# Thresholds of the first 28 steps on VectorE, and tails and second-batch units turned at other steps

## The chip, the cores and the metric

The kernel runs on one core of a Trainium2 chip. The metric is the device time of one execution in microseconds. The numbers here are the median of three runs, and one further execution that the hardware profiler recorded.

## The reference

An attention with a threshold feeds a two-layer perceptron. There are 8 batches of 8 heads, 576 positions and head size 64; q, k and v are float32.

```python
scores = scale * np.matmul(q, k.transpose(0, 1, 3, 2))
thresh = np.max(scores, axis=-1, keepdims=True) - tau
scores = np.where(scores >= thresh, scores, -1000000000.0)
scores = scores - np.max(scores, axis=-1, keepdims=True)
attn = np.exp(scores)
attn = attn / (np.sum(attn, axis=-1, keepdims=True) + 1e-09)
attn_out = np.matmul(attn, v)
# heads side by side: x is 4608 tokens by 512
h = x @ w_in            # 512 by 2048
out = np.maximum(0.01 * h, h) @ w_out   # 2048 by 512
```

So every row of scores needs its maximum, then the comparison with maximum minus tau, the exponential and the row's sum.

## The kernel before, in words

**Steps.** The attention is cut into 144 steps, 18 for each batch. A step handles one pair of heads and 128 queries against all 576 keys. Sixteen of the 18 are main steps: two blocks of 256 queries, four pairs of heads, two halves of the block. The last two take the 64 tail queries (positions 512 to 575) of two pairs each. Everything is issued by one loop over the step number n (lines 544 to 609); each engine has its own queue and runs what the loop gives it in that order. There is no other planner: where something is to happen at a given step, a table keyed by n holds it (`loads_at`, `pool_at`, `turns_at`, `rows_at`).

**One step on the engines.** PE multiplies the scores (line 252) into two PSUM tiles, one a head. VectorE (DVE) copies them to SBUF with the sign turned and keeps each row's least value, which is minus the maximum (line 260, tile `s`, `mn`). The threshold, `mn` plus tau, is a tiny instruction on 128x2 elements (`threshold`, lines 264 to 273): on VectorE it is line 269, and on GpSimd (POOL) line 272. One round of the loop later, ScalarE (ACT) computes, for head 0, an exponential (line 295), and for head 1 a Prelu with the threshold as bias and then an exponential (lines 291 and 292). VectorE multiplies head 0's exponential with the comparison against the threshold (`weights`, line 304). So line 291 and line 304 wait for the threshold. In round n VectorE's queue holds the copies of step n, then the threshold of step n where it is VectorE's, then the weights of step n-1.

**From weights to output.** For each two steps, VectorE takes the reciprocal of the sums (line 310), POOL spreads it over 128 columns (`widen`, line 313), and SyncE (SP) issues one transposing DMA for weights and reciprocals together (line 321). In the first eight steps PE transposes instead. Three to five steps later PE multiplies with v (`pv`, line 348), and VectorE scales the result (line 370, 360 in tail steps). After four pairs the 256 tokens go through the first layer (line 391, PSUM tile `hp`, emptied by ACT in line 393) one eighth a round, and then the second (line 407, two pieces a round at most).

**Splitting and turning q and k.** For precision, q and k are scaled by 64 and split into a high and a low float16 half, and both halves are transposed. A main unit is one pair's 512 positions of q or k; a tails unit is the 64 last positions of all pairs. For most units, POOL scales (line 137), casts (line 143) and subtracts (line 151); `turn` (line 171) lets PE transpose both halves into PSUM (line 186), and VectorE or ACT copies the result to SBUF (line 195 for main units, 189 for tails). For k tails of the second batch POOL makes one more copy (line 191). In the first two batches these run as whole units at steps that the code names; from the third batch on, another form (`turn_rows`) is used.

**PSUM banks that bind.** The tag `h` has two buffers, and `hp`, the transposes of `turn` and a part of the early transposes take them in turn. A new user waits until the one before the last has been emptied.

**What sets the order around the change.** The steps of the second batch's ten units stand in a list in line 450; the split is issued by POOL three and two rounds ahead (lines 452 to 454) and the turn at the round itself (line 456). Units come in the order k and q of pair 0, k tails, k and q of pairs 1, 2 and 3, q tails. The first batch's last units stand in lines 531 to 537: its q tails are split at round 11 and turned at round 13, and first read at step 16. In a round the first entry of `pool_at` is issued ahead of the threshold and the widen, the others behind (lines 566 to 577). The loads of w_in and w_out are in the same table (line 534).

Of the kernel before, what the change touches and what calls it, by code (L numbers as in the profile page):

```python
# [37 lines left out]
def kernel(  # L38
# [35 lines left out]
    def load_main(b, s, which, eng=None, parts=1):  # L74
        t = sb.tile([128, 4, 256], FP32, tag="raw", bufs=4, name="raw")
        n = 4 // parts
        for i in range(parts):
            (eng or nc.sync).dma_start(
                out=t[:, ds(n * i, n), :],
                in_=SRC[which][b, ds(4 * s + n * i, n), 0:MAIN, :].rearrange("h (p t) d -> p h (t d)", t=4))  # L80
        raws[b, s, which] = t

    def load_tails(b, which, engs=(nc.sync, nc.sync)):
        t = sb.tile([128, 2, 2, 64], FP32, tag="rawt", bufs=2, name="rawt")
        src = SRC[which][b, :, MAIN:S, :].rearrange("(u sh) p d -> u p sh d", u=2)
        for u in range(2):
            engs[u].dma_start(out=t[ds(64 * u, 64), :, :, :].rearrange("p s h d -> p (s h) d"), in_=src[u])
        tails[b, which] = t
# [40 lines left out]
    def split_scale(key):  # L129
        t = sb.tile([128, 4, 2, 64], FP32, tag="scaled", bufs=2, name="scaled")  # L130
        if key[1] == "t":
            src = tails[key[0], key[2]][:, :, :, :]
            dst = t[:, 0:2, :, :]
        else:
            src = pair_of(*key)
            dst = t[:, :, :, :].rearrange("p t h d -> p h t d")
        nc.gpsimd.tensor_scalar(out=dst, in0=src, scalar1=64.0, scalar2=1.0, op0=AX.mult, op1=AX.mult)  # L137
        scaled[key] = t

    def split_high(key):  # L140
        n = 2 if key[1] == "t" else 4
        halves[key] = new_half()
        nc.gpsimd.tensor_copy(out=halves[key][:, 0, 0:n, :, :], in_=scaled[key][:, 0:n, :, :])  # L143

    def split_low(key):

        n = 2 if key[1] == "t" else 4
        m = 2 if key[0] < 2 else n
        src = scaled.pop(key)
        for i in range(0, n, m):  # L150
            nc.gpsimd.tensor_tensor(out=halves[key][:, 1, i : i + m, :, :], in0=src[:, i : i + m, :, :],  # L151
                                    in1=halves[key][:, 0, i : i + m, :, :], op=AX.subtract)
# [18 lines left out]
    def turn(key, copy=None, bank="h"):  # L171
        copy = copy or nc.scalar.copy
        b, p, which = key
        dst, half = turned_of(b, which), halves.pop(key)
        n = 2 if p == "t" else 4
        c0 = 0 if which == "q" else 64
        if p == "t":
            c0 = MAIN if which == "q" else 0
            tp = ps.tile([128, 2, 2, 2, 64], FP16, tag=bank, bufs=2 if bank == "h" else 1, name="tp")
        else:  # L180
            tp = ps.tile([128, 2, 4, 128], FP16, tag="h", bufs=2, name="tp")
        for x in range(2):
            for t in range(n):
                for h in range(2):
                    o = tp[ds(64 * h, 64), x, :, t, :] if p == "t" else tp[ds(64 * h, 64), x, t, :]
                    nc.tensor.transpose(o, half[:, x, t, h, :], ident[:, :])  # L186
        if p == "t":
            src = tp[:, :, :, :, :].rearrange("d x u s p -> d x (u s) p")
            copy(out=dst[:, :, :, ds(c0, 64)], in_=src)
            if which == "k" and b:  # L190
                nc.gpsimd.tensor_copy(out=dst[:, :, :, 576:640], in_=dst[:, :, :, 0:64])
            elif which == "k":
                nc.vector.tensor_copy(out=dst[:, :, :, 576:640], in_=src)
        else:
            copy(out=dst[:, :, p, ds(c0, 512)], in_=tp[:, :, :, :].rearrange("d x t p -> d x (t p)"))
# [67 lines left out]

    def threshold(st):
        st.th = sb.tile([128, 2, 2], FP32, tag="th", bufs=3, name="th")
        if st.n < 9 or 15 <= st.n < 23:

            least = sb.tile([128, 1], FP32, tag="least", bufs=2, name="least")
            nc.vector.tensor_scalar(out=st.th[:, :, 0], in0=st.mn[:, :, 0], scalar1=tau_f, scalar2=None, op0=AX.add,
                                    op1=AX.min, accum_out=least[:, :])  # L270
        else:
            nc.gpsimd.tensor_scalar(out=st.th[:, :, 0], in0=st.mn[:, :, 0], scalar1=1.0, scalar2=tau_f, op0=AX.mult,  # L272
                                    op1=AX.add)
# [157 lines left out]
    def at(d, n, f):  # L431
        d.setdefault(n, []).append(f)

    def units(b):
        u = [(b, p, w_) for p in range(NP) for w_ in "kq"]
        return u[:2] + [(b, "t", "k")] + u[2:] + [(b, "t", "q")]
# [3 lines left out]
    for b in range(1, B):  # L440
        base = PERB * (b - 1)
        for i, (s, w_) in enumerate(((0, "k"), (0, "q"), (1, "k"), (1, "q"))):
            at(loads_at, base + ((-2, 0, 5, 7)[i] if b > 1 else (3, 4, 8, 9)[i]),
               lambda b=b, s=s, w_=w_: load_main(b, s, w_))
        for i, w_ in enumerate("kq"):
            at(loads_at, base + (1, 3)[i] if b > 1 else (6, 16)[i], lambda b=b, w_=w_: load_tails(b, w_))
        for i, key in enumerate(units(b) if b == 1 else ROWS):
            n_ = base + (5, 7, 9, 9, 11, 13, 15, 17, 19, 21)[i]
            if b == 1:
                n_ = (11, 12, 13, 14, 16, 17, 19, 20, 21, 22)[i]  # L450
            key = (b,) + key[-2:]
            at(pool_at, n_ - 3, lambda key=key: split_scale(key))
            at(pool_at, n_ - 3, lambda key=key: split_high(key))
            at(pool_at, n_ - 2, lambda key=key: split_low(key))
            if b == 1:
                at(turns_at, n_, lambda key=key, i=i: turn(key, nc.vector.tensor_copy if i < 7 else None))
            else:
                at(rows_at, n_, key)
# [47 lines left out]
    def split_pool(key):  # L506
        split_scale(key)
        split_high(key)
        split_low(key)
# [8 lines left out]
    first = units(0)  # L518
# [8 lines left out]
    for key in first[4:6]:  # L527
        split_high_act(key)
        split_scale(key)
        split_low(key)  # L530
    for n_, key in zip((1, 2, 11), first[7:]):
        at(pool_at, n_, lambda key=key: split_pool(key))
    for i in range(8):
        at(pool_at, i if i < 2 else 1 + i // 2 if i < 6 else i, lambda i=i: load_w(i))
    at(turns_at, 0, lambda: turn(first[3], nc.vector.tensor_copy))
    for n_, key in zip((1, 2, 3, 13), first[5:8] + first[9:]):
        at(turns_at, n_, lambda key=key: turn(key, nc.vector.tensor_copy if key[2] == "q" else None))

    N = len(steps)
# [4 lines left out]
    while n < N + 7 or l1q or l2q or stores:  # L544
# [12 lines left out]
        if n == 0:  # L557
            threshold(steps[0])
# [10 lines left out]
        if 0 < n < N:  # L569
            threshold(steps[n])  # L570
# [72 lines left out]
```

## Time and profile before

| what | value |
|---|---|
| median of 3 runs | 496.63 us (495.94 to 497.31) |
| profiled execution | 495.9 us |
| span of its instructions | 494.1 us |
| PE busy | 476.1 us, 96% of the span |
| VectorE (DVE) busy | 406.9 us, 82% |
| ScalarE (ACT) busy | 433.0 us, 88% |
| GpSimd (POOL) busy | 317.5 us, 64% |
| thresholds on POOL (line 272) | 127 rows, 445 ns each in the mean |
| thresholds on VectorE (line 269) | 17 rows of 0.14 to 0.16 us |
| weights (line 304) | 144 rows, 840 ns each in the mean |

Busy time is the time in which an engine executes instructions; the idle time in front of a row is put down to what released it. The share of a whole span hides that the first 100 us have other limits than the rest, so these are read in windows. The profiled execution's 495.9 us hold 1.8 us outside the span, and lie 0.73 us under the median.

### The profile page before, as it was taken

The numbers are of one execution on the slowest core, as the hardware profiler recorded it, in microseconds if no ns is written. First come the engines' busy times: TensorE is split into PE (matmuls) and PEld (weight loads), VectorE is DVE, ScalarE is ACT, GpSimd is POOL, SyncE is SP. The second block draws the span as 40 slices with busy tenths as digits, with TensorE's granted clock in tenths as the row PEclk, the third lists the DMA queues.
The fourth block names the chain that finished last, engine by engine and source line by source line (L and its number), as shares of the span: only waits on it lengthen the run. The fifth ranks groups of instructions, "written<-read, shape, count | busy, mean of one in ns | idle before, by whom it ended". The sixth has DMA issues, their size and how long they took to land.

```text
span 494.1 us, 19699 instructions
## 1 busy us (share of the span) xinstructions
PE 476.1 (96%) x8039; PEld 344.5 (70%) x8039; DVE 406.9 (82%) x1195; ACT 433.0 (88%) x784; POOL 317.5 (64%) x545
## 2 busy tenths in 40 slices
PE   8888699999999999999999999999999999999996
PEld 7666467667677777777777777777777777667884
DVE  5999698998989898999989898988989898788100
ACT  6999699999999999999999999999999999999431
POOL 5968789877866786667766677677767683222000
PEclk9999899999999999999999999999999999999999
DMA  8998798999999999989997998979988988768512
GB/s 255 262 209 148 144 165 168 207 190 171 238 176 161 224 217 182 184 183 228 156 212 162 220 195 191 211 146 217 180 203 162 200 147 161 124 123 166 106 45 66
DMA packets 220444, 87.79 MB, mean 178 GB/s; under 512 B 190656, under 2 KB 217280, under 8 KB 220352
## 3 DMA queue, kind: packets, MB, share of 16 engines
q1 hardware_dynamic: 217120, 82.00, 81.2%
q0 software_dynamic: 2688, 4.19, 4.9%
q8 instruction: 63, 1.03, 0.8%
q10 hardware_dynamic: 544, 0.33, 0.2%
q14 instruction: 29, 0.24, 0.1%
HBM read 36.70 MB, written 9.44 MB: 93 GB/s over the span
## 4 chain that ended last, share of the span: by engine, by line
PE 81%; DVE 8%; ACT 6%; POOL 2%; issue 1%; DMA 1%; DVEq 0%; POOLq 0%
PE hp L391 26%; PE sc L252 20%; PE o L407 20%; PE pv L348 7%; DVE s L260 4%; PE osc L407 3%; PE tpr L207 3%; DVE w L304 2%; ACT w L292 2%; DMA wT<-w 1%; ACT s L291 1%; ACT e L295 1%; POOL half L151 1%; PE tp L186 1%; PE idle L515 1%
## 5 line engine op out<-in xcount | busy, mean ns | idle before, releaser
L260 DVE TENSOR_SCALAR_CACHE_REDUCE s<-sc 128x576 f32<-128x576 f32 x288 | 206.4, 754 | 35.1 <-PE sc L252 32.7
L391 PE MATMUL hp<-x,win 128*64 128x256 f16 x2048 | 137.6, 277 | 1.1 <-ACT g L393 0.8
L252 PE MATMUL sc<-kT,qT 64*128 64x288 f16 (+1 forms) x1920 | 135.2, 286 | 3.1 <-DVE s L260 1.8
L391 PEld LDWEIGHTS <-win 128*64 128x64 f16 x2560 | 119.2, 110 | 24.5 <-issue 18.5
L407 PE MATMUL o<-wout,g 128*64 128x512 f16 x992 | 127.8, 379 | 0.0
L272 POOL TENSOR_SCALAR th<-mn 128x2 f32<-128x2 f32 x127 | 56.5, 445 | 108.0 <-DVE s L260 80.2
L304 DVE SCALAR_TENSOR_TENSOR w<-s,th,e 128x576 f16<-128x576 f32 x144 | 120.9, 840 | 1.5 <-POOL th L272 1.0
L252 PEld LDWEIGHTS <-qT 64*128 64x128 f16 (+1 forms) x1920 | 76.7, 97 | 57.0 <-issue 41.3
L292 ACT ACTIVATE w<-s,minus_tau 128x576 f16<-128x576 f32 x144 | 111.6, 775 | 4.9
L291 ACT ACTIVATE s<-s,th 128x576 f32<-128x576 f32 x144 | 110.3, 766 | 4.3 <-POOL th L272 3.9
L295 ACT ACTIVATE e<-s,mn 128x576 f16<-128x576 f32 x144 | 110.2, 765 | 1.1 <-DVE s L260 1.1
L393 ACT ACTIVATE g<-hp 128x512 f16<-128x512 f32 x144 | 83.9, 583 | 28.2 <-PE hp L391 27.7
L151 POOL TENSOR_TENSOR half<-scaled,half 128x512 f16<-128x512 f32 (+1 forms) x91 | 88.9, 984 | 2.2
L407 PEld LDWEIGHTS <-g 128*64 128x64 f16 x1152 | 65.3, 110 | 29.8 <-issue 0.2
L348 PE MATMUL pv<-wT,v 128*64 128x256 f16 (+1 forms) x960 | 52.1, 247 | 0.6 <-DMA wT<-w 0.5
L348 PEld LDWEIGHTS <-v 128*64 128x64 f16 x960 | 41.3, 111 | 14.5 <-DVE s L260 1.0
L137 POOL TENSOR_SCALAR scaled<-raw 128x512 f32<-128x512 f32 x62 | 45.1, 728 | 5.3 <-DMA raw<-in_k_dram 4.0
L143 POOL CAST half<-scaled 128x512 f16<-128x512 f32 (+1 forms) x74 | 42.7, 577 | 4.5
L313 POOL CAST w<-rec 128x256 f16<-128x256 f32 (+1 forms) x70 | 31.4, 449 | 12.5 <-DVE rec L310 11.7
L106 POOL CAST v<-vraw 128x256 f16<-128x256 f32 x64 | 31.7, 524 | 1.3
L370 DVE TENSOR_TENSOR x<-pv,wT 128x256 f16<-128x256 f32 x64 | 27.0, 422 | 4.6 <-PE pv L348 3.9
L292 ACT ACTIVATION_READ_ACCUMULATOR w<-s,minus_tau 128x1 f32 x144 | 26.9, 187 | 0.0
(55 smaller groups left out, 320.9 us busy)
## 6 DMA issues: line engine op xcount, KB each, us to landing
vraw<-in_v_dram SPq DMA_DIRECT2D x16, 512.0 KB, 5.1
out_dram<-osb SPq DMA_DIRECT2D x16, 512.0 KB, 3.3
raw<-in_k_dram SPq DMA_DIRECT2D x14, 512.0 KB, 4.6
raw<-in_q_dram SPq DMA_DIRECT2D x14, 512.0 KB, 4.9
win<-in_moe_w_in_dram POOLq DMA_DIRECT2D x4, 512.0 KB, 7.3
wout<-in_moe_w_out_dram POOLq DMA_DIRECT2D x4, 512.0 KB, 13.8
wT<-w SPq DMA_TRANSPOSE x68, 6.0
raw<-in_k_dram SPq DMA_DIRECT2D x4, 256.0 KB, 4.6
```

The source lines that it names most:

```text
L151: nc.gpsimd.tensor_tensor(out=halves[key][:, 1, i : i + m, :, :], in0=src[:, i : i + m, :, :], in1=halves[key][:, 0, i : i + m, :, :], op= ...
L252: nc.tensor.matmul(out=o, lhsT=lhs, rhs=turned[st.b, "k"][rows, kx, pair, ds(key0, 288)], start=(i == 0), stop=(i == 2), skip_group_check= ...
L260: nc.vector.tensor_scalar(out=st.s[:, h, :].rearrange("p (a b) -> p a b", a=2), in0=st.sc[h][:, :, 0:288], scalar1=-1.0 / UNIT, scalar2=No ...
L272: nc.gpsimd.tensor_scalar(out=st.th[:, :, 0], in0=st.mn[:, :, 0], scalar1=1.0, scalar2=tau_f, op0=AX.mult, op1=AX.add)
L291: nc.scalar.activation(out=z, in_=z, func=AF.Prelu, bias=st.th[:, h, 0:1], scale=-1.0, alpha=1e20)
L292: nc.scalar.activation(out=st.w[h], in_=z, func=AF.Exp, bias=minus_tau[:, :], scale=1.0, accum_out=st.sum[h])
L295: nc.scalar.activation(out=st.e[:, :], in_=st.s[:, h, :], func=AF.Exp, bias=st.mn[:, h, 0:1], scale=-1.0)
L304: nc.vector.scalar_tensor_tensor(out=st.w[0], in0=st.s[:, 0, :], scalar=st.th[:, 0, 0:1], in1=st.e[:, :], op0=AX.is_le, op1=AX.mult, accum ...
L348: nc.tensor.matmul(out=o, lhsT=v16[st.b % 2][:, 2 * c + u if st.tail else st.p, blk, :], rhs=rhs, start=(i == 0), stop=(i == 4), skip_grou ...
L391: nc.tensor.matmul(out=hp[ds(64 * u2, 64), jj, :], lhsT=w_in16[:, i, ds(128 * j + 64 * u2, 64)], rhs=g.x[:, i, :], start=(i == 0), stop=(i ...
L393: nc.scalar.activation(out=g.g[:, ds(nj * u, nj), :], in_=hp[:, :, :], func=AF.Prelu, bias=0.0, scale=1.0, alpha=0.01)
L407: nc.tensor.matmul(out=g.o[ds(64 * u2, 64), :], lhsT=g.g[:, j, ds(128 * m + 64 * u2, 64)], rhs=w_out16[:, j, :], start=(j == 0), stop=(j = ...
```

## The change

Three things are changed, and only in numbers of steps. The thresholds of steps 9 to 14 and 23 to 27 go from POOL to VectorE, so that VectorE has all of the first 28. The first batch's q tails are split at round 7 instead of 11 and turned at round 10 instead of 13. Of the second batch's units, k tails turn at round 14 instead of 13, k of pair 1 at 15 instead of 14, q of pair 1 at 17 instead of 16 and k of pair 2 at 18 instead of 17; their splits on POOL move with them, by one round each.

```diff
     def threshold(st):
         st.th = sb.tile([128, 2, 2], FP32, tag="th", bufs=3, name="th")
-        if st.n < 9 or 15 <= st.n < 23:
+        if st.n < 28:
...
             if b == 1:
-                n_ = (11, 12, 13, 14, 16, 17, 19, 20, 21, 22)[i]
+                n_ = (11, 12, 14, 15, 17, 18, 19, 20, 21, 22)[i]
...
-    for n_, key in zip((1, 2, 11), first[7:]):
+    for n_, key in zip((1, 2, 7), first[7:]):
         at(pool_at, n_, lambda key=key: split_pool(key))
...
-    for n_, key in zip((1, 2, 3, 13), first[5:8] + first[9:]):
+    for n_, key in zip((1, 2, 3, 10), first[5:8] + first[9:]):
         at(turns_at, n_, lambda key=key: turn(key, nc.vector.tensor_copy if key[2] == "q" else None))
```

The number of instructions is the same but for the thresholds: a threshold on VectorE also has a read of its accumulator. The order on ACT and on SP does not change. On POOL, eleven thresholds go, the first batch's q tails stand ahead of the last load of w_out, and the four moved units stand one round later.

## The prediction

> **What bounds the kernel now.** I read the page first, then the chain that ended last, then the busy time of each engine in windows, and then the timeline of each engine around the one window that differs.
>
> ```profile
> span 494.1 us, 19699 instructions
> PE 476.1 (96%) x8039; PEld 344.5 (70%) x8039; DVE 406.9 (82%) x1195; ACT 433.0 (88%) x784; POOL 317.5 (64%) x545
> ...
> PE 81%; DVE 8%; ACT 6%; POOL 2%; issue 1%; DMA 1%; DVEq 0%; POOLq 0%
> ```
>
> PE carries the kernel. In the chain in order of time, though, VectorE and ScalarE hold most of the first 73 us; from "73.47 PE sc L252" on it is nearly all PE, and the windows from 108 to 456 us show PE full. So work that gets PE to that point earlier shortens the whole, and the first 73 us are where this change acts. Windows there (columns: length; busy time of PE, PEld, DVE, ACT, POOL; granted clock; DMA share; GB/s):
>
> ```profile
> 40.00:50.00 10.00, 9.05 (x147) 6.95 (x145) 9.78 (x25) 8.93 (x16) 9.10 (x16) 1.00 0.78 134
> 50.00:60.00 10.00, 6.18 (x90) 4.35 (x86) 6.26 (x18) 6.24 (x11) 7.73 (x15) 0.83 0.83 141
> 60.00:72.00 12.00, 11.12 (x213) 8.58 (x210) 11.78 (x39) 11.56 (x21) 9.47 (x13) 1.00 0.80 153
> ```
>
> Around it DVE is 98% busy and sets the pace. In 50 to 60 us every engine loses a third. The timelines of POOL, ACT, PE and DVE (start, length, engine, line, what, idle before):
>
> ```profile
> 48.30 0.91 POOL L137 TENSOR_SCALAR scaled<-rawt 128x256 f32<-128x256 f32 x1
> 49.27 0.40 POOL L143 CAST half<-scaled 128x256 f16<-128x256 f32 x1
> 49.76 1.92 POOL L151 TENSOR_TENSOR half<-scaled,half 128x256 f16<-128x256 f32 x3
> 51.76 0.19 POOL L272 TENSOR_SCALAR th<-mn 128x2 f32<-128x2 f32 x1
> ```
> ```profile
> 51.99 0.78 ACT L291 ACTIVATE s<-s,th 128x576 f32<-128x576 f32 x1 [2.28 <-POOL th L272]
> ```
> ```profile
> 49.96 0.42 PE L186 MATMUL tp<-ident,half 128*64 128x128 f16 x8
> 54.20 0.41 PE L186 MATMUL tp<-ident,half 128*64 128x128 f16 x8 [3.81 <-ACT g L393]
> 54.54 1.62 PE L252 MATMUL sc<-kT,qT 64*128 64x288 f16 x12
> 56.09 1.92 PE L391 MATMUL hp<-x,win 128*64 128x256 f16 x16
> ```
> ```profile
> 51.99 1.27 DVE L304 SCALAR_TENSOR_TENSOR w<-s,th,e 128x576 f16<-128x576 f32 x1 [0.99 <-POOL th L272]
> 54.65 0.42 DVE L189 COPY qT<-tp 128x512 f16<-128x512 f16 x1 [1.05 <-PE tp L186]
> 56.27 0.76 DVE L260 TENSOR_SCALAR_CACHE_REDUCE s<-sc 128x576 f32<-128x576 f32 x1 [1.20 <-PE sc L252]
> ```
>
> Read as one chain: at step 12 POOL stands behind the q tails' split (L137, L143, one L151), so the threshold comes at 51.76, though its minimum was there by 48; ACT's Prelu and DVE's weights wait for it; ACT's g, behind the Prelu, empties an h bank 2.3 us late; the second tail transpose of step 13 needs that bank, so PE stands 3.81 us. Then its rows are slow: 12 score matmuls take 1.62 us (0.91 elsewhere) and 16 hp matmuls 1.92 (1.06), at a mean granted clock of 0.83.
>
> The Trainium skill (TensorE: Matmul & The Clock Gate, Part 1) says that an idle window of about 3.4 us halves PE's clock until a busy one has passed. The 3.81 us and the slow rows agree.
>
> **The change part by part.** I price on DVE, which sets the pace up to step 20, from the start of one step's first L260 copy to the next: step 9 at 38.38, 10 at 40.77, 43.60, 46.35, 49.48, 14 at 56.27, 59.98, 62.74, 65.97, 69.10, 71.99, and 20 at 74.88. That is 36.50 us for eleven steps. Costs by start-to-start times: the two copies 1.35 (38.38 to 39.73); reciprocal 0.09; weights L304 0.74 to 1.2; a main unit's copy L195 0.60 (45.75 to 46.35); 128x512 L189 or L370 0.34.
>
> *Thresholds 9 to 14 to DVE.* Alone, one delays L304 by 0.20 (36.25 to 36.45 at step 8, nothing at step 9); behind a reciprocal 0.10 (67.33 to 67.52 against 44.95 to 45.04). Even steps 0.20, odd 0.10, but step 10's copies waited 0.22 for PE, which covers step 9's. POOL loses six rows (0.19 to 0.62) and the waits for DVE before them; ACT's 0.67 and 2.28 and DVE's 0.99 waits on them go.
>
> *First batch's q tails, 11 to 7 (split) and 13 to 10 (turn).* POOL's scale 0.40, cast 0.40 and subtract about 0.7 enter the 3.86 us that it stands before its row at 35.12; the raw tails were issued by 10.2 us and landed within 9.4. The last w_out load, on POOL's queue behind them, starts 1.6 us later, at about 32; its first reader is the o row at 69.18. The eight transposes (0.3) go to PE in step 10, where PE waits for DVE at the next scores anyway; the copy adds 0.34 to DVE there. SP's order is as before.
>
> *Second batch's units.* k tails go from 13 to 14, k pair 1 to 15, q pair 1 to 17, k pair 2 to 18, each with scale, cast, subtracts and transposes, the tails with their POOL copy L191 too. Earliest reader: step 18 for the tails, 20 for pair 1, 22 for pair 2. On POOL the k tails' cast now stands behind step 11's widen, which waits for a reciprocal near 45.6; POOL can afford that wait there. No step then has two turns, so the bank conflict is gone. DVE's copies move with them.
>
> Steps 9 to 19 afterwards: 2.39; 2.83+0.20+0.34 = 3.37; 2.75+0.10 = 2.85; 3.13+0.20 = 3.33; step 13 without turns would be 1.35+0.19+0.74..1.19, but ACT needs about 2.75 a step (its e, s, w and g rows 0.68+0.80+0.78+0.48; its e rows at 46.23 and 48.94 lie 2.71 apart), so 2.75; step 14: 1.35+0.20+0.74+0.34+0.34 = 2.97; step 15: 1.35+0.19+0.98+0.60 = 3.12; step 16 on ACT again 2.75; 3.13; 2.89+0.60 = 3.49; 2.89. Sum 33.04 against 36.50: **3.46 us gained at step 20**. PE has room: its fullest step, 18, holds 0.84 scores, 0.99 hp, 0.47 tp, 0.86 o and 0.65 pv = 3.81, and step 19, without hp and pv, gives that back.
>
> *What is late next.* POOL, no longer held up, is full from about 56 us: its copy L191 waits for DVE's k tails copy of step 14 (53.1+1.35+0.20+0.82+0.34, near 55.9), and all of k pair 2 now lies behind that. From there L191 0.6, q pair 1's subtracts 1.3, a widen 0.4, k pair 2 1.1+0.7+1.5 and q pair 2 0.7+0.7+1.6 bring it to 64.5, so step 17's widen (L313) starts 1.1 us behind its reciprocal (before: at once) and ends near 64.9. The transpose issued there took 7.56 us to land, against 7.64 to its pv at 75.63: no slack. The pv of step 20 then falls at about 72.2 and the data at 72.5: 0.25 lost, between 0 and 1.5 (L151's spread 1.3 to 1.9 over three units).
>
> *Thresholds 23 to 27 to DVE.* DVE is full only in 25 to 27 (90.60 to 99.16). There 0.1+0.2+0.1 delays the pv evacuation that PE waits 0.42 for at 96.34, about 0.3. But POOL's widen of step 27 stood behind a threshold (97.99, then 98.24), the transpose behind it landed 0.52 late for PE at 105.83, and without that threshold it starts about 0.25 earlier. I take 0; ends -0.5 (the whole wait goes) and +1.0 (five at 0.20, all on the path).
>
> *Unseen: meetings of L304 with POOL.* L304 takes 0.81 clear of POOL's L137 and L143 and 1.02 to 1.27 over them. In the eleven steps it sums to 10.9 us; all clear it would be 8.9, all at 1.27 14.0: ends -2.0 and +3.1. By my row-by-row placing step 9 meets more and 10, 12 and 13 less; I take 0.
>
> Sum: 3.46 - 0.25 = **3.2 us**. The profiled execution took 495.9 us (span 494.1 and 1.8 around it), so 492.7; it lies 0.73 under the median of 496.63, so 493.4.
>
> **The rivals.**
> 1. POOL becomes the limiter: freed of waits, it has a unit (0.7+0.7+1.3 at least) in nearly every step of about 3 us, every widen comes a micro-second or so late, and pv waits at steps 20, 22 and 24. For it: the transposes for pv at 75.63 and 88.91 had no slack already. Against: before step 17's widen POOL stood 1.91 us. Price 1.5: 494.9. Chance 0.14.
> 2. Every L304 meets a POOL split: +3.1, 496.5, no difference to be measured. The row at 51.99 is one such; that five of the eleven take 0.82 or less speaks against. Chance 0.06. The Trainium skill (SBUF — State Buffer, where the diagram of the doors is read) says that the pair shared by both is an exclusive lock and the later one blocks. That points this way; taken whole, the trace agrees only in part, as 0.46 is the most a meeting cost, less than a 0.61 split.
> 3. Slower: PE's clock drops at the thinned steps 13 to 16. There PE has 2.1 to 2.8 us of work a step with gaps of up to 0.7. At the slow rates (sc +0.7, hp +0.9) a step grows by about 1.2 beyond its gap; from the third such step on the gain is gone, and four cost 4.8: 496.6 - 3.2 + 4.8 = 498.2. Against: the clock was 1.00 from 28 to 50 us with like gaps (0.75 at 27.34). With DVE pressed beyond my rows in 23 to 27 included, chance 0.10.
> 4. Meetings fall away: -2.0, 491.4. Chance 0.09.
>
> **How the numbers follow.** My forecast (492 to 494.5) has 0.61 of the chances. About 0.3%, 1.5 us, is what a measurement can tell from no change. Faster: 0.61+0.14+0.09 = 0.84; same 0.06; slower 0.10. The range 491.0 to 496.0 takes in the first, second and most of the fourth case, and leaves out the third and the collisions.
>
> **What would show it.** In the new trace: PE rows of step 13 without the 3.81 us wait and the granted clock 1.00 throughout; no wait of ACT's L291 on POOL between 40 and 57 us; step 20's first L260 near 71.5; L269 rows 0.15 long at each step; a wait of PE at pv step 20 on the transpose of 0 to 1.5 us. I am wrong if step 20 comes at 71.5 and the end does not follow (PE then loses it behind a transpose), or if L304 rises above 1.05 on average in steps 9 to 19.

## The result, and the profile after

The changed kernel took 492.38 us in the median of six runs (492.15 to 492.81); the kernel before, beside it, 496.77 us (495.94 to 497.31). The ratio is 0.9913, with a 95% interval of 0.990 to 0.9926: 4.4 us, or 0.9%, faster. The forecast was 493.4 us, 3.2 us faster, with a range of 491.0 to 496.0.

The page of the changed kernel, its span, busy times and the chain that ended last by engine:

```profile
span 490.3 us, 19692 instructions
PE 475.4 (97%) x8039; PEld 343.6 (70%) x8039; DVE 406.9 (83%) x1217; ACT 432.7 (88%) x784; POOL 315.2 (64%) x534
...
PE 78%; DVE 9%; ACT 4%; POOL 4%; DMA 2%; issue 2%; SPq 0%; POOLq 0%; DVEq 0%; ACTq 0%
```

No engine has less to do worth speaking of (PE 0.7 us, POOL 2.3 us); what went is waiting. Windows of the changed kernel around the place of the old stall (length; busy PE, PEld, DVE, ACT, POOL; granted clock; DMA share; GB/s):

```profile
40.00:50.00 10.00, 9.26 (x149) 6.97 (x150) 9.74 (x35) 9.90 (x18) 7.60 (x11) 1.00 0.86 148
50.00:56.00 6.00, 4.94 (x82) 3.76 (x80) 5.81 (x21) 5.79 (x12) 3.48 (x6) 1.00 0.69 133
56.00:68.00 12.00, 11.46 (x222) 8.69 (x218) 11.93 (x40) 11.44 (x22) 11.55 (x17) 1.00 0.96 188
```

DVE is now 97% busy or more in all three, the granted clock is 1.00, and POOL, with 3.48 of 6 us of work in the second window, is full in the third. The rows that answer to the chain shown of before, in the timelines of ACT, PE and DVE (start, length, engine, line, what, idle before):

```profile
49.27 0.76 ACT L291 ACTIVATE s<-s,th 128x576 f32<-128x576 f32 x1
```
```profile
51.07 0.28 PE L252 MATMUL sc<-kT,qT 64*128 64x288 f16 x1 [0.66 <-DVE s L260]
51.75 0.89 PE L252 MATMUL sc<-kT,qT 64*128 64x288 f16 x11 [0.40 <-DVE s L260]
52.57 1.06 PE L391 MATMUL hp<-x,win 128*64 128x256 f16 x16
53.47 0.39 PE L186 MATMUL tp<-ident,half 128*64 128x128 f16 x8
```
```profile
51.73 0.15 DVE L269 TENSOR_SCALAR_CACHE_REDUCE th<-mn 128x2 f32<-128x2 f32 x1
51.81 0.81 DVE L304 SCALAR_TENSOR_TENSOR w<-s,th,e 128x576 f16<-128x576 f32 x1
52.79 0.76 DVE L260 TENSOR_SCALAR_CACHE_REDUCE s<-sc 128x576 f32<-128x576 f32 x1 [0.15 <-PE sc L252]
```

The Prelu has no wait, PE's longest wait there is 0.66 us and is for VectorE's copies, and score and hp rows take their usual 0.9 and 1.06 us. Step 14 starts at 52.79 instead of 56.27.

The difference of the two spans by stretches, from the first L260 copy of one step to that of another:

| stretch | before | after | difference |
|---|---|---|---|
| start to step 8 | 34.91 | 35.37 | +0.46 |
| step 8 | 3.47 | 3.29 | -0.18 |
| steps 9 to 19 | 36.50 | 32.13 | -4.37 |
| steps 20 to 35 | 48.17 | 48.70 | +0.53 |
| steps 36 to 142 | 330.49 | 330.20 | -0.29 |
| step 143 to the end | 40.58 | 40.57 | -0.01 |

Nearly all of the gain arises in steps 9 to 19, and some of it is lost again in the sixteen steps behind. The first row is not the change: over the fourteen profiled executions of this study, whose programs differ ahead of step 8 by the q tails' split at most, step 8 starts between 34.48 and 36.04 us.

The place of the loss is seen in PE's timeline, and its cause in POOL's:

```profile
85.36 0.74 PE L348 MATMUL pv<-wT,v 128*64 128x256 f16 x10 [0.52 <-DMA wT<-w]
```
```profile
76.52 0.61 POOL L143 CAST half<-scaled 128x512 f16<-128x512 f32 x1
77.22 1.16 POOL L151 TENSOR_TENSOR half<-scaled,half 128x512 f16<-128x512 f32 x1
78.32 0.93 POOL L313 CAST w<-rec 128x256 f16<-128x256 f32 x1
```

The reciprocal for the widen at 78.32 (step 21) was done by 75.0. POOL stood in splits until then; the transpose behind it was issued at 79.27 and landed at 85.31, and the pv of step 24 waited for it.

### The profile page after: what moved, and what is told of

Same layout as the page of the kernel before. It is cut to its first block, busy times and chain, and to the rows that moved or that the text cites. A ratio compares the mean times of both kernels' runs of the same rounds, so it can differ in the third digit from the quotient of the medians.

```text
span 490.3 us, 19692 instructions
## 1 busy us (share of the span) xinstructions
PE 475.4 (97%) x8039; PEld 343.6 (70%) x8039; DVE 406.9 (83%) x1217; ACT 432.7 (88%) x784; POOL 315.2 (64%) x534
## 3 DMA queue, kind: packets, MB, share of 16 engines
q8 instruction: 63, 1.03, 0.9%
## 4 chain that ended last, share of the span: by engine, by line
PE 78%; DVE 9%; ACT 4%; POOL 4%; DMA 2%; issue 2%; SPq 0%; POOLq 0%; DVEq 0%; ACTq 0%
PE hp L391 25%; PE o L407 20%; PE sc L252 20%; PE pv L348 7%; DVE s L260 5%; PE osc L407 4%; PE tpr L207 3%; DVE w L304 2%; POOL half L151 1%; DMA wT<-w 1%; DMA raw<-in_q_dram 1%; ACT w L292 1%; ACT e L295 1%; ACT s L291 1%; DVE x L370 1%
## 5 line engine op out<-in xcount | busy, mean ns | idle before, releaser
L260 DVE TENSOR_SCALAR_CACHE_REDUCE s<-sc 128x576 f32<-128x576 f32 x288 | 206.4, 753 | 33.4 <-PE sc L252 31.4
L304 DVE SCALAR_TENSOR_TENSOR w<-s,th,e 128x576 f16<-128x576 f32 x144 | 120.3, 835 | 0.5 <-ACT e L295 0.5
L272 POOL TENSOR_SCALAR th<-mn 128x2 f32<-128x2 f32 x116 | 52.7, 454 | 103.0 <-DVE s L260 81.2
L151 POOL TENSOR_TENSOR half<-scaled,half 128x512 f16<-128x512 f32 (+1 forms) x91 | 89.3, 987 | 2.3
L143 POOL CAST half<-scaled 128x512 f16<-128x512 f32 (+1 forms) x74 | 44.6, 602 | 4.5
L137 POOL TENSOR_SCALAR scaled<-raw 128x512 f32<-128x512 f32 x62 | 43.6, 702 | 5.4 <-DMA raw<-in_k_dram 4.4
```

Of the source, the lines that this page charges most:

```text
L260: nc.vector.tensor_scalar(out=st.s[:, h, :].rearrange("p (a b) -> p a b", a=2), in0=st.sc[h][:, :, 0:288], scalar1=-1.0 / UNIT, scalar2=No ...
L304: nc.vector.scalar_tensor_tensor(out=st.w[0], in0=st.s[:, 0, :], scalar=st.th[:, 0, 0:1], in1=st.e[:, :], op0=AX.is_le, op1=AX.mult, accum ...
```

## The experiments

**Which of the three parts does it.** Three runs each do one part alone, and a fourth leaves out the thresholds 23 to 27.

```diff
-        if st.n < 9 or 15 <= st.n < 23:
+        if st.n < 23:
```

> The kernel before with one part alone: thresholds 9 to 14 on VectorE (condition n < 23). Theory (one chain, every link needed): the threshold of step 12 comes at about 48 instead of 51.76, ACT's g empties its bank near 51.2, PE stands about 1.2 us at the second tails turn instead of 3.81, its clock stays at 1.00, step 14's first copy starts 3.3 to 3.7 us earlier than in the kernel before, and the whole is 3 to 4 us faster: about 493.3. Rival (the bank alone: two turns behind one another are the cause): PE still stands over 3 us at the second turn and the gain is under 1 us: about 496. Rival (POOL's load is shared out, each of the three parts brings a third): about 495.3.

Measured: 492.03 us against 496.55 beside it, ratio 0.9907 (0.9894 to 0.992). PE's timeline has the second turn with a third of the old wait, and the granted clock was 1.00 in this stretch:

```profile
51.89 0.41 PE L186 MATMUL tp<-ident,half 128*64 128x128 f16 x8 [1.32 <-ACT g L393]
```

```diff
-    for n_, key in zip((1, 2, 11), first[7:]):
+    for n_, key in zip((1, 2, 7), first[7:]):
...
-    for n_, key in zip((1, 2, 3, 13), first[5:8] + first[9:]):
+    for n_, key in zip((1, 2, 3, 10), first[5:8] + first[9:]):
```

> The kernel before with one part alone: the first batch's q tails split at 7 and turned at 10; thresholds and second batch as before. Theory (one chain): no second turn at step 13 and no tails' split in front of step 12's threshold, so PE's 3.81 us wait goes although thresholds stay on POOL; ACT still waits about 1 us for a threshold. Step 14's first copy 3 to 4 us earlier than before, whole 493 to 494. Rival (the thresholds on POOL are the cause): ACT's wait stays over 2 us, gain under 1 us: about 496. Rival (each part a third): about 495.3.

Measured: 492.58 us, 0.9917 (0.9905 to 0.993). The late threshold remains as a wait of ACT, but nothing passes it on to PE (timeline of ACT):

```profile
50.56 0.77 ACT L291 ACTIVATE s<-s,th 128x576 f32<-128x576 f32 x1 [0.73 <-POOL th L272]
```

```diff
-                n_ = (11, 12, 13, 14, 16, 17, 19, 20, 21, 22)[i]
+                n_ = (11, 12, 14, 15, 17, 18, 19, 20, 21, 22)[i]
```

> The kernel before with one part alone: the second batch's units at the new steps (k tails 14, k of pair 1 15, q of pair 1 17, k of pair 2 18). Theory (one chain): step 13 then has only the first batch's q tails' turn, whose bank is free early, so PE's long wait goes; the threshold of step 12 is still late by about 1.5 us behind the q tails' split. Step 14's first copy 2.5 to 3.5 us earlier, whole 493.3 to 494.5. Rival (thresholds on POOL are the cause): about 496. Rival (each part a third): about 495.3.

Measured: 493.18 us, 0.9928 (0.9915 to 0.9941). Steps 9 to 19 take 32.13 us, as in the changed kernel, but steps 20 to 35 take 49.40, with pv waiting for transposes:

```profile
71.85 0.74 PE L348 MATMUL pv<-wT,v 128*64 128x256 f16 x10 [1.08 <-DMA wT<-w]
79.06 0.82 PE L348 MATMUL pv<-wT,v 128*64 128x64 f16 x40 [0.41 <-DMA wT<-w]
```

The threshold of step 12 came at 49.07 in this run, 1.7 us behind its minimum instead of 4.0, and ACT's Prelu did not wait for it.

```diff
-        if st.n < 28:
+        if st.n < 23:
```

> The changed kernel with thresholds 23 to 27 back on POOL (condition n < 23). Theory: the 0.6 us that the changed kernel loses between steps 23 and 26 come from POOL's late widen of step 21 and the transpose behind it (pv of step 24 waited 0.52 us), which this does not touch: 492.4, within 0.4 us of the changed kernel, and the pv wait stays. Rival (VectorE, pressed by the five thresholds, loses them): 0.4 to 0.8 us faster than the changed kernel, 491.7.

Measured: 492.05 us, 0.9908 (0.9894 to 0.9922); 0.3 us under the changed kernel's median, less than the intervals tell apart. Waits of pv on transposes stay (0.27 us at step 24, 0.26 at step 28, 0.68 at step 30).

What follows: with the first part alone PE's wait of 3.81 us shrinks to 1.32, with the second or the third alone it is gone, and each part brings 3.4 to 4.5 us, somewhat more than was expected of it. The first part takes away the threshold's lateness and leaves the second turn. The other two take away the second turn and most of the lateness with it, so no run shows what the second turn costs without a late threshold, or the full lateness without a second turn. The thirds of the second rival, and the single causes of the first, are refuted: they gave 495.3 and 496. All three together are not better than the first alone, as far as the intervals tell. The stretches say the same: steps 9 to 35 take 80.82 us with the first alone and 80.83 with all three, as what is gained ahead of step 20 is lost behind it.

**What the slow clock cost.** The kernel before, with PE kept busy in the stall:

```diff
-        for f in turns_at.get(n, []):
+        for i, f in enumerate(turns_at.get(n, [])):
+            if n == 13 and i == 1:
+                idle(50)
             f()
```

> The kernel before, with 50 idle matmuls (128x128, results unused) on PE between the two tails' turns of step 13, so that PE is busy through most of the 3.81 us stall; nothing else changed. Theory (the slow clock after the stall costs something of its own): step 14's first copy stays near 56.3, the score rows behind it take 0.91 instead of 1.62 and the hp rows 1.06 instead of 1.92, step 14 shortens from 3.70 to 3.0 to 3.2, and the whole is 0.3 to 0.7 us faster than the kernel before: about 496.1. Rival (VectorE's pace hides the slow clock): granted clock 1.00, and the time within 0.2 us of the kernel before.

Measured: 495.64 us against 497.36 beside it, 0.9969 (0.9956 to 0.9981). PE's timeline:

```profile
51.34 2.96 PE L515 MATMUL idle<-ident 128*128 128x128 f16 x50
55.24 0.41 PE L186 MATMUL tp<-ident,half 128*64 128x128 f16 x8 [0.93 <-ACT g L393]
55.59 0.91 PE L252 MATMUL sc<-kT,qT 64*128 64x288 f16 x12
56.42 1.06 PE L391 MATMUL hp<-x,win 128*64 128x256 f16 x16
```

The turn still has to wait for its bank, but the rows behind it run at full speed. Step 13 falls from 6.79 to 6.09 us and step 14 from 3.70 to 3.03; 0.36 is given back at step 16. The profiled execution reached step 8 1.03 us later than that of the kernel before, so the two are compared by stretches: steps 9 to 19 are 1.07 us shorter, about a quarter of what the change gains there, and more than was expected. The rival, that VectorE's pace hides the clock, is refuted. The Trainium skill (TensorE: Matmul & The Clock Gate, Part 1) has the clock fall after an idle window of about 3.4 us; this run agrees, as with 0.93 us of idle left the granted clock was 1.00 throughout.

**Where the rest of the gain goes.** These runs start from the changed kernel and take away what makes POOL's widens late in steps 17 to 21. First the second batch's casts of v:

```diff
-            at(pool_at, 2 + p if b == 0 else base + (19 if b == 1 else 15) + 2 * p, lambda b=b, p=p: cast_v(b, p))
-        at(pool_at, 2 if b == 0 else base + (19 if b == 1 else 16), lambda b=b: cast_vtails(b))
+            at(pool_at, 2 + p if b == 0 else ((12, 14, 23, 25)[p] if b == 1 else base + 15 + 2 * p), lambda b=b, p=p: cast_v(b, p))
+        at(pool_at, 2 if b == 0 else base + (21 if b == 1 else 16), lambda b=b: cast_vtails(b))
```

> The changed kernel with the second batch's casts of v moved on POOL: pairs 0 and 1 from steps 19 and 21 to 12 and 14, where POOL waited 1.0 and 1.4 us, and the tails from 19 to 21 behind the widen. Theory (POOL's late widen of step 21 makes pv of step 24 wait): that widen starts 1.5 to 2.3 us earlier against its reciprocal, the 0.52 us wait at pv 24 goes, and the whole is 0.3 to 0.6 us faster than the changed kernel: about 491.9. Rival (the transposes themselves are the wall, whatever POOL does): the wait turns up at the pv of step 26, 28 or 30 and the whole stays within 0.2 us of the changed kernel: 492.3.

Measured: 492.05 us against 497.36, 0.9898 (0.9883 to 0.9912). The widen of step 21 starts at 76.47, 1.8 us behind its reciprocal (74.67) instead of 3.3; pv of step 24 starts at 84.67 without a wait, and steps 20 to 35 take 48.30 us.

Then the widen of step 21 alone on VectorE:

```diff
-            widen(ended[0], 0, 2)
+            widen(ended[0], 0, 2, nc.vector if n == 21 else None)
```

> The changed kernel with one widen, that of step 21, on VectorE instead of POOL. Theory (POOL's late widen of step 21 makes pv of step 24 wait): it comes about 3 us earlier, the 0.52 us wait at pv 24 goes, VectorE pays about 0.35 us in a step in which it also waits for PE, and the whole is 0.2 to 0.5 us faster than the changed kernel: about 492.0. Rival (the transposes themselves are the wall): a wait of about 0.5 us at a later pv, up to step 30, and 492.3.

Measured: 491.54 us, 0.9883 (0.9868 to 0.9898). In its profiled execution pv of step 24 has no wait, but those of steps 20 and 22 wait 0.57 and 0.48 us, and steps 20 to 35 take 48.73 us, as in the changed kernel. The trace does not show where the faster median is from. Its interval lies just under that of the changed kernel (0.990 to 0.9926), but the two were not measured beside each other.

Then the moved casts, the widens of 17, 19 and 21 on VectorE, and thresholds 23 to 27 on POOL:

```diff
-        if st.n < 28:
+        if st.n < 23:
...
-            widen(ended[0], 0, 2)
+            widen(ended[0], 0, 2, nc.vector if n in (17, 19, 21) else None)
```

> The changed kernel with the casts of v moved as in the run with moved casts, the widens of steps 17, 19 and 21 on VectorE, and thresholds 23 to 27 back on POOL. Theory (what is lost from step 18 to 30 is POOL's lateness): no pv before step 30 waits for a transpose, the lead of 4.9 to 5.5 us that the variants have near step 18 is kept to more than 4.5 at step 36, and the whole takes about 491.5. Rival (the transposes are the wall): the lead at step 36 is again 3.3 to 3.7, with waits of pv on transposes that were issued right behind their reciprocals, and 492.2.

Measured: 492.69 us, 0.9909 (0.9895 to 0.9922). No pv before step 30 waits, and steps 20 to 35 take 47.94 us, the least of all; but steps 9 to 19 take 33.17 us, 1.04 more than in the changed kernel, so the lead of 4.5 us at step 36 did not come (3.99, with a start 0.25 early). Two of the three widens fall into those steps, and the L304 there sum to 10.40 us instead of 9.72. Neither expectation fits the whole: late widens are a loss, but here VectorE paid for them with as much.

**The thresholds by themselves, and the comparison on one chip.** The two moves without any threshold moved:

```diff
-        if st.n < 28:
+        if st.n < 9 or 15 <= st.n < 23:
```

> The two moves without the thresholds: tails at 7 and 10, units at the new steps, thresholds 9 to 14 and 23 to 27 on POOL as in the kernel before. Theory (the thresholds on VectorE pay for themselves because POOL's splits, no longer held up, meet fewer of VectorE's L304): the eleven L304 of steps 9 to 19 sum to 10.9 us or more instead of 9.7, which costs what the six missing thresholds save; steps 9 to 19 take 32.0 to 32.8 us and the whole is within 0.7 us of the changed kernel. Rival (the thresholds on VectorE are a plain cost of 1 us): steps 9 to 19 take about 31.2 us, and the whole is 1 us faster than the changed kernel.

Measured: 492.94 us against 496.64, 0.9923 (0.9904 to 0.9943). Steps 9 to 19 take 31.57 us: 0.56 less than with the thresholds on VectorE, about half of what the rival expected. The eleven L304 sum to 9.98 us, so the theory's reason, longer L304, was wrong. Steps 20 to 35 take 50.12, and the whole is no faster. PE's timeline:

```profile
72.12 0.74 PE L348 MATMUL pv<-wT,v 128*64 128x256 f16 x10 [1.49 <-DMA wT<-w]
79.76 0.82 PE L348 MATMUL pv<-wT,v 128*64 128x64 f16 x40 [0.84 <-DMA wT<-w]
```

So what the missing thresholds save ahead of step 20 is lost behind it, at transposes. Beside it ran three more:

> The changed kernel itself, as the comparison on this chip for the three beside it. 4.0 to 4.8 us faster than the kernel before on this chip; steps 9 to 19 in 32.1 us, the pv of step 24 waiting about 0.5 us for its transpose.

Measured: 492.98 us, 0.9924 (0.9908 to 0.994). Steps 9 to 19 take 32.14 us, as expected. But in this execution three pv wait, not one (steps 20, 22 and 24), and steps 20 to 35 take 49.22 us, with the same program:

```profile
71.95 0.74 PE L348 MATMUL pv<-wT,v 128*64 128x256 f16 x10 [0.53 <-DMA wT<-w]
79.20 0.82 PE L348 MATMUL pv<-wT,v 128*64 128x64 f16 x40 [0.45 <-DMA wT<-w]
86.03 0.74 PE L348 MATMUL pv<-wT,v 128*64 128x256 f16 x10 [0.37 <-DMA wT<-w]
```

So between single traces, differences of half a micro-second in steps 20 to 35 say nothing by themselves.

The kernel with moved casts, unchanged from the run above:

> The run with moved casts of v once more, now on one chip beside the changed kernel. Theory (POOL's late widen of step 21 costs the changed kernel its wait at pv 24): 0.3 to 0.7 us faster than the changed kernel beside it, steps 20 to 36 about 48.2 us against 48.7. Rival: within 0.2 us.

Measured: 492.48 us, 0.9912 (0.9895 to 0.9928): 0.5 us under the changed kernel beside it. Steps 20 to 35 take 48.56 us against 49.22. Step 24 has no wait; steps 20 and 22 do (PE's timeline, then POOL's widen of step 21):

```profile
71.15 0.74 PE L348 MATMUL pv<-wT,v 128*64 128x256 f16 x10 [0.43 <-DMA wT<-w]
78.40 0.82 PE L348 MATMUL pv<-wT,v 128*64 128x64 f16 x40 [0.38 <-DMA wT<-w]
84.69 0.71 PE L348 MATMUL pv<-wT,v 128*64 128x256 f16 x10
```
```profile
76.25 0.39 POOL L313 CAST w<-rec 128x256 f16<-128x256 f32 x1
```

And moved casts with the widen of step 21 on VectorE (both diffs above):

> The changed kernel with the casts of v moved and also the widen of step 21 on VectorE. Theory (each of the two already brings that transpose in time): no gain on top of the moved casts, since step 21's widen no longer holds up any pv; about 0.2 to 0.4 us slower than moved casts alone, as VectorE pays about 0.35, and 0.2 faster than the changed kernel. Rival (earlier is better, whatever waits): 0.3 us or more faster than moved casts alone.

Measured: 492.15 us, 0.9909 (0.9891 to 0.9927), 0.8 us under the changed kernel and 0.3 under moved casts alone; its steps 20 to 35 take 48.37 us. That points to the rival, but the intervals overlap: not settled.

What follows: the moved casts take away the wait of step 24 in both executions and were 0.5 us faster than the changed kernel on one chip. The intervals overlap, and the six times of each overlap a little too (491.59 to 492.91 us against 492.61 to 493.68), so a version that beats it is likely, not proved.

## Why the prediction was right

**The chain and the stall: right.** Its place, its links and its end were as told. Runs that take them out show the threshold's lateness and the slow clock; the second turn went only together with most of the lateness, and that ACT's g stands behind the Prelu is read from ACT's rows. That PE carries the lead from step 36 on is right as well: 330.49 and 330.20 us.

**Steps 9 to 19, 3.46 us forecast, 4.37 measured: mis-sized.** By step, in us:

| step | 9 | 10 | 11 | 12 | 13 | 14 | 15 | 16 | 17 | 18 | 19 |
|---|---|---|---|---|---|---|---|---|---|---|---|
| forecast | 2.39 | 3.37 | 2.85 | 3.33 | 2.75 | 2.97 | 3.12 | 2.75 | 3.13 | 3.49 | 2.89 |
| measured | 2.52 | 2.97 | 2.89 | 3.23 | 2.52 | 2.97 | 2.89 | 2.62 | 2.89 | 3.29 | 3.33 |

Two terms failed. The eleven L304 were taken as unchanged at 10.9 us; they sum to 9.72, as nine of them now take 0.81 or 0.82 (the others 1.15 and 1.24), against five before. The fourth rival had this as a case of its own, with 2.0; it was 1.2. But its reason, meetings that fall away, is not what happened: in the kernel before all eleven L304 overlap a row of POOL, in the changed one ten. What counts is which of the two starts first, as two meetings of the changed kernel show (DVE, then POOL, each time):

```profile
40.21 0.81 DVE L304 SCALAR_TENSOR_TENSOR w<-s,th,e 128x576 f16<-128x576 f32 x1
40.29 1.20 POOL L143 CAST half<-scaled 128x512 f16<-128x512 f32 x1
69.01 1.24 DVE L304 SCALAR_TENSOR_TENSOR w<-s,th,e 128x576 f16<-128x576 f32 x1
69.03 0.61 POOL L143 CAST half<-scaled 128x512 f16<-128x512 f32 x1
```

Where POOL's row starts 0.07 us or more behind L304, L304 keeps its 0.81 and POOL's row grows, here from 0.61 to 1.20. Where POOL's row starts within 0.04 us of it or a few tenths ahead, it is mostly L304 that grows. From step 8 on, the fourteen executions have 983 L304 with no row of POOL under way at their start or beginning within 0.05 us of it, and all of them take 0.78 to 0.82 us, whatever starts behind. The subtracts do it too: in the kernel before the L304 at 42.13 took 1.20 over two L151, so the prediction's reading, that L137 and L143 lengthen it, was too narrow. What set the order in which the two engines started is not shown.

The other term is ACT, taken as a floor of 2.75 for steps 13 and 16, which took 2.52 and 2.62. ACT's rate binds a run of steps, not a single one behind which it may fall back a little: its e rows at 48.60, 51.38 and 54.17 lie 2.78 and 2.79 apart, while VectorE's steps 12 to 14 take 3.23, 2.52 and 2.97. Against these stand step 19, whose L304 rose from 0.81 to 1.24, and step 9. The thresholds cost what was priced where they can be read: step 14 is exact, and without the threshold it takes 2.90 with an L304 longer by 0.13, which leaves 0.20 for the threshold.

**What is late next, 0.25 us at the pv of step 20: the right mechanism, the wrong place and too small.** POOL ends step 17's widen at 65.14 (64.9 forecast), but it started 1.95 us behind its reciprocal, not 1.1. The transpose behind it was taken at 7.56 us to landing and took 5.86 and 6.59 in the two executions; the two errors work against each other. In the first execution it landed at 71.03 and pv started without a wait:

```profile
71.11 0.71 PE L348 MATMUL pv<-wT,v 128*64 128x256 f16 x10
```

The pv of step 24 waited instead. In the second, steps 20, 22 and 24 waited 0.53, 0.45 and 0.37. Steps 20 to 35 became 0.53 and 1.05 us longer than before. More was gained in steps 9 to 19 than forecast (0.9 us) and more was lost behind them (0.3 to 0.8); that these misses partly cancel, so that the total came out 1.2 us from the forecast, is luck.

**Thresholds 23 to 27, taken as 0: not told apart from 0** by the run without them (0.3 us, within the intervals).

**The rivals.** POOL as limiter is a loss of half a micro-second to one, not 1.5, but the waits that it named, at the pv of steps 20, 22 and 24, are those of the second execution. Nearly every L304 does meet a row of POOL, as the second rival has it, but only two of eleven are longer for it. In the kernels without the stall, and in the one with the stall filled, the granted clock was 1.00 up to the last 2 us of the span. Of the signs that were named, step 20's first copy came at 70.79 instead of 71.5, and L304 takes 0.88 us in the mean of steps 9 to 19, well under 1.05.

## What to carry to other kernels

A long wait on the bounding engine can be the end of a chain of small ones, and taking out one of them can free nearly all of it; three edits then brought no more than one, as far as these runs tell. Where two engines hold each other up, look at which starts first, not at how often they overlap. What the freed engines do next decides how much is kept: look for the in-order queue that the waits had given slack (here POOL's, in front of the transposes), and price it from that queue's own rows. Compare by stretches between fixed points of the program, since the start alone varied by 1.5 us.

## What was not expected of the hardware

The slow clock behind a stall of 3.81 us cost 1.07 us on top of it, even where another engine set the pace. And the same program, executed twice, had its transposes late at one pv or at three: that of step 17 took 5.86 us from issue to landing in one execution (65.17 to 71.03) and 6.59 in the other (65.31 to 71.90), which is the difference between no wait and 0.53 us. Last, the long thresholds on POOL are meetings with L304 too: in the kernel before, 75 of 127 start inside an L304, take 0.57 to 0.63 us and end 0.05 us behind its end, and the other 52 take 0.19. That is what the mean of 445 ns is made of.
